# Runs in the evictions of q and k, value copies one unit later, a slot list in smaller doses and GpSimd in a pinned order

## The chip, the cores and the metric

The kernel runs on one core of a Trainium2 chip. The metric is device time in microseconds (us); lower is better. Three runs of the kernel before were timed, and one more execution was recorded with a profile.

## What is computed

Eight batches of banded attention are followed by a mixture of experts in which every token goes to one expert.

```python
# attention: B, H, S, D = 8, 8, 576, 64; heads 0-3: plain window of 32; heads 4-7: every 4th key of 128
scores = q @ k.T / 8; scores outside the band are masked; attn = softmax(scores)
x = (attn @ v) laid out as [B*S, H*D] = [4608, 512]
# experts: E = 8, F = 1024
logits = x @ w_gate + modality_bias[modality_id]
e = argmax(logits); g = softmax(logits)[e]
out = g * (relu(x @ w1[e]) @ w2[e])
```

## The kernel before

**Attention.** A batch is nine units (m = 0 to 8): four units of two tiles of 64 queries for the plain heads (kind 0), one mixed unit, and four units for the dilated heads (kind 1). One loop over t = 9b + m issues, at each t, a stage of several units: the scores of unit t (TensorE into the one tile `pss`, then VectorE adds the mask and takes the maximum, GpSimd subtracts it in `sm`), the exponent of unit t-1 (ScalarE), the transposition of the probabilities of t-2 (TensorE, evicted by ScalarE to `pT`), the product with the values of t-3 (`attend`, TensorE), the normalising and storing of t-3 and t-4 and the router's logits of t-5. ScalarE, VectorE, TensorE and SyncE (SP, which issues the loads) each run their instructions strictly in the order in which this loop writes them. GpSimd's order was left to a scheduler, apart from chains that were declared.

**q and k of the next batch** come as `st` tiles and are transposed in six chunks (`qk_chunks`), one for q and one for k in each of the three units m = 4, 5, 6 (kind 0) and m = 8, 0, 1 (kind 1). A chunk is four TensorE transpositions into one PSUM tile and one ScalarE eviction (two for kind 1) to `kT` or `qT`. In `qT` and `kT` the token p*6 + s lies at its own place, so the 96 columns of one transposition (one s) go to places six elements apart.

**Values.** `load_v` brings 64 rows of each tile to partitions 32 to 95 of `vw`; `shift_v`, a ScalarE copy of 32x520 for each head, copies the last 32 rows of each tile to the partitions 0 to 31 of the next one. `attend` of unit m = 0 runs at t with m = 3, that of unit m = 4 at m = 7.

**Experts.** From batch 4 on three early slots of up to 256 tokens are formed; the slots numbered 0 to 2 here. After the last batch the full list of slots is made (`gating`, `slot_info`, `slot_list`, `rest_info`: some 45 small VectorE instructions on one partition, run as a generator, a step for each `advance()`), and 15 more full slots and one half slot follow. A slot has 8 steps f. Each step is 12 matmuls with `w1` (L854), a ReLU (`hh` on ScalarE, `hl` on VectorE), splits of the next weights (`w1h`, `w2h` on ScalarE, `w1l`, `w2l` on VectorE, L802 and L803) and 6 matmuls with `w2` (L834). The tokens of a slot come through a chain: their indices (`idt`, a load by SP that needs the list), four indirect gathers by GpSimd into the one tile `xr`, a store to `x_slot` by SP, four loads into the one tile `xg` by SP, two transpositions `xt` by VectorE with splits `xh` (ScalarE) and `xl` (VectorE). The weights of the next slot are loaded by SP in six pieces, each of which waits until its place was used: `w2q` pair 0, `w1q` half 0, pairs 1 and 2, half 1, pair 3. `hold` at a slot's start issues what is missing of its inputs before its first matmul. After the loop over t, a short loop issues steps of the experts and of the list until the list is there (`state['routed']`).

Of the kernel before, what the change touches and what calls it, by code (L numbers as in the profile page):

```python
# [22 lines left out]
B, H, S, D = 8, 8, 576, 64  # L23
# [10 lines left out]
PQ = 96  # L34
SI = S // PQ
# [29 lines left out]
def kernel(  # L65
# [12 lines left out]
    nc = tc.nc  # L78
# [30 lines left out]
    def vw(b, kd):  # L109
        return vws[(2 * b + kd) % 3]  # L110

    def load_one(b, kd, src, queue=nc.sync):

        t = ald.tile([PQ, SI, 4, D], F32, name="st")
        for h in range(4):
            queue.dma_start(out=t[:, :, h], in_=src[b, 4 * kd + h].rearrange("(p s) d -> p s d", s=SI))
        return t

    def load_qk(b, kd, queue=nc.sync):
        kn = load_one(b, kd, k)  # L120
        return load_one(b, kd, q, queue), kn

    def load_v(b, kd, part=slice(None)):

        t = vw(b, kd)
        if kd == 0:
            nc.sync.dma_start(out=t[WIN:KW, :, :, 0:D], in_=v[b, 0:4].rearrange("h (i p) d -> p h i d", p=TQ))
        else:
            vv = v[b, 4:8].rearrange("h (j r) d -> r j h d", r=NCLS)
            for i, o, r, j, n in [(i, *seg) for i in range(NTILE) for seg in _csegs(TQ * i, TQ * (i + 1))][part]:  # L130
                nc.sync.dma_start(out=t[WIN + o:WIN + o + n, :, i, 0:D], in_=vv[r, j:j + n])
        return t

    def shift_v(b, kd, h):

        t = vw(b, kd)
        nc.scalar.copy(out=t[0:WIN, h, 1:NTILE].rearrange("p i d -> p (i d)"), in_=t[TQ:KW, h, 0:NTILE - 1].rearrange("p i d -> p (i d)"))

    state = {('qk', 0, 0): load_qk(0, 0, nc.scalar)}
# [3 lines left out]
    ident = cpool.tile([P, P], F32, name="ident")  # L143
# [125 lines left out]
    class InOrder:  # L269


        def __getattr__(self, name):
            def issue(*args, **kw):
                ins = tc.keep_in_program_order(getattr(nc.gpsimd, name)(*args, **kw))  # L274
                state['pool'] = ins.ins
                return ins
            return issue

    pool = InOrder()


    def qk_chunks(kd, qn, kn):


        def chunk(n, is_q):
            src = qn if is_q else kn
            pt = psum['o'].tile([P, 512], F32, name="po") if is_q and psum['many'] else ps_t.tile([P, 512], F32, name="pt")
            for g in range(2):
                for i in range(2):
                    nc.tensor.transpose(out=pt[:, PQ * (2 * g + i):PQ * (2 * g + i + 1)],  # L290
                                        in_=src[:, 2 * n + i, 2 * g:2 * g + 2].rearrange("p a d -> p (a d)"), identity=ident[:PQ, :PQ])
            flat = qT[kd] if is_q else kT[kd][:, :, WIN:]
            inp = pt[:, 0:4 * PQ].rearrange("c (g i p) -> c g i p", g=2, p=PQ)
            if kd == 0:
                parts = [(flat.rearrange("c g (p s) -> c g s p", s=SI)[:, :, 2 * n:2 * n + 2], inp)]
            else:

                parts = []
                for e in range(2):
                    o = 6 * e + 2 * n  # L300
                    dst = flat.rearrange("c g (r j t) -> c g r t j", r=NCLS, t=3)[:, :, o % 4:o % 4 + 2, o // 4]
                    parts.append((dst, inp.rearrange("c g i (j e) -> c g i e j", e=2)[:, :, :, e]))
            for dst, src in parts:
                if is_q:
                    nc.scalar.mul(dst, src, 1.0 / 8.0)
                else:
                    nc.scalar.copy(out=dst, in_=src)
        return [(lambda n=n, is_q=is_q: chunk(n, is_q)) for n in range(SI // 2) for is_q in (False, True)]
# [363 lines left out]
    order = []  # L672
# [4 lines left out]
    NU = len(order)  # L677
# [245 lines left out]
    def step(share=MOE_RATE / 6):  # L923

        nonlocal credit
        if moe:
            credit += share if state['t'] < NU else 1
            while credit >= 1:
                credit -= 1
                next(moe, None)  # L930

    def advance(some=range(-1, B)):
        for b, task in tasks:
            if b in some:
                next(task, None)

    state['routed'] = False
    for t in range(NU + LAG + 1):
        state['t'] = t
        if 'go' in state and not moe:  # L940
            octx.close()
            psum['many'] = False
            psum['y'] = ctx.enter_context(tc.tile_pool(name="ps_y", bufs=2, space=PSUM))
            psum['o'] = ctx.enter_context(tc.tile_pool(name="ps_o1", bufs=1, space=PSUM))
            moe = slots(NS, ids_of, ahead, hold)
        b, m = t // 9, t % 9
        if t == 1:
            pieces = qk_chunks(1, *state['qk', 0, 1])
        if t < NU:
            jobs = order[t][1]  # L950
            if m == 0:
                state['lT', b] = gwk.tile([2 * NE, S], F32, name="lT")
            if b + 1 < B:
                if m == 4:
                    pieces = qk_chunks(0, *state['qk', b + 1, 0])
                elif m == 8:
                    pieces = qk_chunks(1, *state['qk', b + 1, 1])
            if m == 0 and b > 0:
                load_v(b, 1, slice(6, None))
            elif m == 3:  # L960
                if b + 1 < B:
                    state['v', b + 1, 0] = load_v(b + 1, 0)
            units.append(Unit(b, m, jobs, [state['v', b, 0], state['v', b, 1]] if m >= 4 else [state['v', b, 0]], state['lT', b]))
            units[t].scores()
        step()
        if 0 <= t - 1 < NU:
            units[t - 1].exp()
        po = psum['o'].tile([P, 512], F32, name="po")
        if 0 <= t - 3 < NU:
            units[t - 3].attend(po)  # L970
        step()
        if 0 <= t - LAG < NU:
            units[t - LAG].logits(po)
        if 0 <= t - 3 < NU:
            units[t - 3].normalize()
        if 0 <= t - LAG < NU:
            units[t - LAG].gather_logits()
            if (t - LAG) % 9 == 8:
                tasks.append(((t - LAG) // 9, background((t - LAG) // 9)))
        step()  # L980
        advance()
        if 0 <= t - 2 < NU:
            units[t - 2].probsT()
        step()
        if 0 <= t - 4 < NU:
            units[t - 4].store()
            units[t - 4].keep(pool)

        if 3 <= m <= 6 and b < B:
            shift_v(b, 1, m - 3)  # L990
        elif t < NU and (m == 8 and b + 1 < B or m < 3):
            for h in ((m + 1) % 9,) if t > 2 else {0: (0, 1), 1: (2, 3), 2: ()}[t]:
                shift_v(b + (m == 8), 0, h)
        for i in range(2):
            step()
            if i < len(pieces):
                pieces[i]()
        pieces = pieces[2:]
        if t < NU and b + 1 < B:

            if m == 1:
                state['k', 1] = load_one(b + 1, 1, k)
            elif m == 2:
                state['qk', b + 1, 1] = load_one(b + 1, 1, q), state['k', 1]
            elif m == 6 and b + 2 < B:
                state['k', 0] = load_one(b + 2, 0, k)
            elif m == 7 and b + 2 < B:
                state['qk', b + 2, 0] = load_one(b + 2, 0, q), state['k', 0]
            elif m == 8:
                state['v', b + 1, 1] = load_v(b + 1, 1, slice(0, 6))  # L1010
        advance([*round_of, B - 1] if moe and t < NU else range(-1, B))


    while not state['routed']:
        step(1)
        advance()
        advance()
    run(moe)
    man.close()
# [34 lines left out]
```

## Time and profile before

| | |
|---|---|
| runs | 710.84, 721.43, 710.94 us; median 710.94 us |
| profiled execution | 717.6 us; span 715.9 us, so 1.7 us lie around the span |
| busy: TensorE, VectorE, ScalarE, GpSimd | 652.0, 496.2, 455.5, 290.7 us |
| granted TensorE clock, mean | 0.954 |

In the rows PE is TensorE's matmuls, PEld its weight loads, DVE VectorE, ACT ScalarE, POOL GpSimd, and SPq SyncE's queue. A row of the timeline gives start and duration in us, engine, line, operation, output <- inputs, shapes and count, and in brackets the idle time before it with what ended it. Attention fills about the first 258 us; the experts' slots start there and repeat every 22.56 us once they run alone.

### The profile page before, as it was taken

Reading aid. Unit: us, or ns where it says so; the run is one execution under the profiler, and the core shown is the slowest. Engines: PE = TensorE matmul, PEld = TensorE weight load, DVE = VectorE, ACT = ScalarE, POOL = GpSimd, SP = SyncE. Lnnn points to the kernel's source line nnn. Section 1 sums busy time; section 2 is a strip of 40 time slices with the busy share of each in tenths; the row PEclk is TensorE's granted clock in tenths of the full one; section 3 lists DMA queues with packets and bytes.
Section 4 is the critical chain, followed back from the end, with each engine's and each line's share of the span. In section 5 each row is a group of like instructions: output and inputs, shape, how many; then the busy total and the mean of one; then the engine's idle time right before and its main releaser. Section 6 shows DMA issues by size and latency. Waiting matters only on the chain. (4 is left out here: it accounts for less than half of the span.)

```text
span 715.9 us, 17885 instructions
## 1 busy us (share of the span) xinstructions
PE 652.0 (91%) x6286; PEld 572.8 (80%) x6286; DVE 496.2 (69%) x1212; ACT 455.5 (64%) x964; POOL 290.7 (41%) x396
## 2 busy tenths in 40 slices
PE   6898899996988789879999999999999999999991
PEld 3687777775876578779999989999999899999880
DVE  1678788785787788687666766677666776667660
ACT  4698799895767665436656555656665565665650
POOL 7344766764658654433333232333213231310110
PEclk7699999999789899989999999999999999999996
DMA  9897698697856964213333863233232336821730
GB/s 163 144 224 176 156 193 177 136 189 131 166 123 159 242 161 79 89 51 98 118 108 100 247 170 115 75 104 119 73 106 75 104 118 169 220 82 46 197 90 12
DMA packets 163233, 94.95 MB, mean 133 GB/s; under 512 B 124144, under 2 KB 143090, under 8 KB 163140
## 3 DMA queue, kind: packets, MB, share of 16 engines
q1 hardware_dynamic: 146612, 63.89, 40.1%
q0 software_dynamic: 11120, 28.64, 13.2%
q10 hardware_dynamic: 5408, 1.24, 1.1%
q8 instruction: 51, 0.84, 0.5%
q14 instruction: 42, 0.34, 0.2%
HBM read 127.52 MB, written 29.39 MB: 219 GB/s over the span
## 5 line engine op out<-in xcount | busy, mean ns | idle before, releaser
L854 PE MATMUL pt<-xh,w1l 128*128 128x256 f32 (+1 forms) x608 | 172.6, 284 | 7.5 <-DVE w1l L803 7.5
L854 PE MATMUL pt<-xl,w1h 128*128 128x256 f32 (+1 forms) x608 | 172.1, 283 | 0.0
L854 PE MATMUL pt<-xh,w1h 128*128 128x256 f32 (+1 forms) x608 | 172.0, 283 | 0.0
L860 ACT ACTIVATE hh<-pt 128x256 fp32r<-128x256 f32 (+1 forms) x152 | 57.6, 379 | 160.3 <-PE pt L854 160.2
L803 DVE TENSOR_TENSOR w2l<-w2q,w2h 128x512 fp32r<-128x512 f32 x152 | 104.8, 689 | 43.1 <-ACT w2h L802 34.7
L274 POOL DMA_INDIRECT xr<-x_dram,idt x74 | 82.8, 1118 | 121.4 <-DMA x_slot<-xr 70.5
L854 PEld LDWEIGHTS pt<-xh,w1l 128*128 128x128 f32 x608 | 116.5, 192 | 8.4 <-DVE w1l L803 8.4
L854 PEld LDWEIGHTS pt<-xh,w1h 128*128 128x128 f32 x608 | 116.4, 191 | 7.2 <-ACT w1h L802 0.6
L854 PEld LDWEIGHTS pt<-xl,w1h 128*128 128x128 f32 x608 | 116.4, 191 | 5.7
L834 PE MATMUL py<-w2h,hh 128*128 128x512 f32 x296 | 118.3, 400 | 0.0
L834 PE MATMUL py<-w2h,hl 128*128 128x512 f32 x296 | 117.2, 396 | 0.0
L834 PE MATMUL py<-w2l,hh 128*128 128x512 f32 x296 | 116.2, 393 | 0.0
L861 DVE SCALAR_TENSOR_TENSOR hl<-pt,hh 128x256 fp32r<-128x256 f32 (+1 forms) x152 | 63.2, 416 | 74.9 <-ACT hh L860 74.9
L274 POOL DMA_INDIRECT out_dram<-ys,idt x37 | 39.8, 1076 | 178.7 <-ACT ys L837 115.8
L803 DVE TENSOR_TENSOR w1l<-w1q,w1h 128x512 fp32r<-128x512 f32 x152 | 103.8, 683 | 3.0 <-ACT w1h L802 3.0
L802 ACT CAST w1h<-w1q 128x512 fp32r<-128x512 f32 x152 | 94.5, 622 | 3.6 <-DMA w1q<-in_moe_w_dram 3.6
L802 ACT CAST w2h<-w2q 128x512 fp32r<-128x512 f32 x152 | 93.1, 612 | 0.0
L274 POOL TENSOR_TENSOR sm<-sm,nmx 128x384 f32<-128x384 f32 x72 | 59.9, 832 | 64.4 <-DVE den L368 49.3
L361 PE MATMUL po<-vw,pT 96*64 96x65 f32 x1152 | 55.9, 239 | 20.3 <-ACT pT L355 16.5
L361 PEld LDWEIGHTS po<-vw,pT 96*64 96x64 f32 x1152 | 44.6, 147 | 32.7 <-ACT pT L355 20.9
L834 PEld LDWEIGHTS py<-w2l,hh 128*128 128x128 f32 x296 | 55.9, 189 | 13.3
L834 PEld LDWEIGHTS py<-w2h,hh 128*128 128x128 f32 x296 | 56.4, 190 | 6.7
(160 smaller groups left out, 1119.9 us busy)
## 6 DMA issues: line engine op xcount, KB each, us to landing
w2q<-in_moe_w_dram SPq DMA_DIRECT2D x76, 512.0 KB
w1q<-in_moe_w_dram SPq DMA_DIRECT2D x152, 256.0 KB
st<-in_k_dram SPq DMA_DIRECT2D x64, 144.0 KB
x_slot<-xr SPq DMA_DIRECT2D x18, 512.0 KB
xg<-x_slot SPq DMA_DIRECT2D x72, 128.0 KB
x_dram<-x_sb POOLq DMA_DIRECT2D x32, 256.0 KB, 3.6
st<-in_q_dram SPq DMA_DIRECT2D x56, 144.0 KB
vw<-in_v_dram SPq DMA_DIRECT2D x8, 576.0 KB
```

Source lines behind the costliest of these rows:

```text
L274: ins = tc.keep_in_program_order(getattr(nc.gpsimd, name)(*args, **kw))
L361: nc.tensor.matmul(out=pov[u * TQ:(u + 1) * TQ, h, :], lhsT=self.pT[:, h, u * TQ:(u + 1) * TQ], rhs=self.vts[kd][:, h, i, :], start=True, ...
L802: nc.scalar.copy(out=hi, in_=raw)
L803: nc.vector.tensor_tensor(out=lo, in0=raw, in1=hi.bitcast(F32), op=ALU.subtract)
L834: nc.tensor.matmul(out=py[u], lhsT=ht[:, us], rhs=wt, start=(f + n == 0), stop=(f + n == FC + 1))
L854: nc.tensor.matmul(out=ph, lhsT=wt[:, c, :], rhs=xt[:, c, 0:cols], start=(c + i == 0), stop=(c + i == KC + 1))
L860: nc.scalar.activation(out=hh, in_=ph, func=AF.Relu)
L861: nc.vector.scalar_tensor_tensor(out=hl, in0=ph, scalar=0.0, in1=hh.bitcast(F32), op0=ALU.max, op1=ALU.subtract)
```

## The change

There are four edits.

1. **Evictions of kind 0.** The four transpositions of a chunk write PSUM with a step of 4 (or 2) elements, so that four (two) tokens that are neighbours in `qT`/`kT` lie beside each other. The eviction reads PSUM in one contiguous run and writes runs of 4 (2) elements, still at a step of six from run to run. The chunks 0 and 1 take one pair of heads each with s = 0 to 3, chunk 2 both pairs with s = 4, 5; before, every chunk took both pairs with two s. Kind 1 keeps its patterns.
2. **Value copies.** For kind 0 the four copies stood at m = 8, 0, 1, 2 and stand at m = 0, 1, 2, 2; for kind 1 they stood at m = 3, 4, 5, 6 and stand at m = 4, 5, 6, 6.
3. **Slot list.** The last loop issued one step of the experts and two of the list at a time; now it is three steps of the experts and one of the list.
4. **GpSimd.** Each instruction issued through `pool` is tied behind the one before it in the scheduler's eyes. No semaphore is added.

```diff
         def __getattr__(self, name):
             def issue(*args, **kw):
                 ins = tc.keep_in_program_order(getattr(nc.gpsimd, name)(*args, **kw))
+                if 'pool' in state:
+                    tc.add_manual_dep(ins.ins, state['pool'].name, mybir.DependencyInfo(mybir.DependencyClass.NoSync, mybir.DependencyReason.SCHED_ONLY),
+                                      reason="GpSimd's order")
                 state['pool'] = ins.ins
...
-            for g in range(2):
-                for i in range(2):
-                    nc.tensor.transpose(out=pt[:, PQ * (2 * g + i):PQ * (2 * g + i + 1)],
-                                        in_=src[:, 2 * n + i, 2 * g:2 * g + 2].rearrange("p a d -> p (a d)"), identity=ident[:PQ, :PQ])
             flat = qT[kd] if is_q else kT[kd][:, :, WIN:]
-            inp = pt[:, 0:4 * PQ].rearrange("c (g i p) -> c g i p", g=2, p=PQ)
+            inp = pt[:, 0:4 * PQ]
             if kd == 0:
-                parts = [(flat.rearrange("c g (p s) -> c g s p", s=SI)[:, :, 2 * n:2 * n + 2], inp)]
+                gs, s0, ns = ((n,), 0, 4) if n < 2 else ((0, 1), 4, 2)
+                inp = inp.rearrange("c (g p i) -> c g p i", g=len(gs), i=ns)
+                jobs = [(inp[:, x, :, i], s0 + i, g) for x, g in enumerate(gs) for i in range(ns)]
+                parts = [(flat[:, gs[0]:gs[-1] + 1].rearrange("c g (p s) -> c g p s", s=SI)[:, :, :, s0:s0 + ns], inp)]
...
+            for to, i, g in jobs:
+                nc.tensor.transpose(out=to, in_=src[:, i, 2 * g:2 * g + 2].rearrange("p a d -> p (a d)"), identity=ident[:PQ, :PQ])
...
-        if 3 <= m <= 6 and b < B:
-            shift_v(b, 1, m - 3)
-        elif t < NU and (m == 8 and b + 1 < B or m < 3):
-            for h in ((m + 1) % 9,) if t > 2 else {0: (0, 1), 1: (2, 3), 2: ()}[t]:
-                shift_v(b + (m == 8), 0, h)
+        for h in {0: (0,), 1: (1,), 2: (2, 3)}.get(m, ()) if 2 < t < NU else {0: (0, 1), 1: (2, 3)}.get(t, ()):
+            shift_v(b, 0, h)
+        for h in {4: (0,), 5: (1,), 6: (2, 3)}.get(m, ()) if t < NU else ():
+            shift_v(b, 1, h)
...
     while not state['routed']:
-        step(1)
-        advance()
+        for _ in range(3):
+            step(1)
         advance()
```

What this does to the order of the engines is shown at three places.

GpSimd in batch 7, before: `sm` is the subtraction that the softmax of a unit waits for, `xr` are the gathers of slot 1, `table` a scatter of the router.

```order
L274 DMA x_dram_84<-x_sb 64x256
L274 DMA x_dram_85<-x_sb 64x256
L493 DMA table<-pay,dst 41472x3
L274 DMA xr<-x_dram_84,idt 128x256
L274 DMA xr<-x_dram_85,idt 128x256
L274 DMA xr<-x_dram_84,idt 128x256
L274 TENSOR_TENSOR sm<-sm,nmx 128x384
```

The same engine after the change, at the end of batch 7, where the last `sm` of all stands:

```order
L274 TENSOR_TENSOR sm<-sm,nmx 128x384
L274 DMA x_dram_84<-x_sb 64x256
L274 DMA x_dram_85<-x_sb 64x256
L274 DMA xr<-x_dram_84,idt 128x256
L274 DMA xr<-x_dram_85,idt 128x256
L274 DMA xr<-x_dram_84,idt 128x256
L274 DMA xr<-x_dram_85,idt 128x256
```

The gathers of slot 1 have moved from ahead of subtractions, with nine subtractions still to come, to behind the last one.

VectorE in slot 1, before, where the list is computed (`w2l` and `w1l` are the splits that the matmuls need, `hl` the VectorE half of a ReLU, the rest belongs to the list):

```order
L548 SCALAR_TENSOR_TENSOR cs<-one_277,ns 1x8
L559 TENSOR_TENSOR ge<-sidx,cs 1x200
L561 TENSOR_REDUCE es<-ge 1x25
L563 TENSOR_TENSOR ns<-full,done 1x8
L565 TENSOR_TENSOR ge<-ge,ns 1x200
L567 TENSOR_REDUCE bs<-ge 1x25
```

The same instructions after the change, at the end of slot 1 (the first `hl` here is that of its step 7, the second that of step 0 of slot 2):

```order
L555 SCALAR_TENSOR_TENSOR cs<-one_277,ns 1x8
L868 SCALAR_TENSOR_TENSOR hl<-pt,hh 128x256
L566 TENSOR_TENSOR ge<-sidx,cs 1x200
L568 TENSOR_REDUCE es<-ge 1x25
L570 TENSOR_TENSOR ns<-full,done 1x8
L810 TENSOR_TENSOR w2l<-w2q_245,w2h 128x512
L810 TENSOR_TENSOR w1l<-w1q_240,w1h 128x512
L868 SCALAR_TENSOR_TENSOR hl<-pt,hh 128x256
```

The list stood in two blocks around the `hl` of step 3 of slot 1, 30 instructions of it in the second; now 2 to 14 of them stand between one `hl` and the next. The list of the full slots is complete behind the `hl` of step 1 of slot 2, where it was complete ahead of the `hl` of step 4 of slot 1.

SP before, where the tokens of slot 3 (the first slot that needs the list) are stored; `w2q_245` is pair 3 of slot 2's weights, and the `idt` here is that of slot 5:

```order
L665 DMA w2q_245<-in_moe_w_dram 128x2x512
L620 TENSOR_LOAD info_5924
L620 ISA x2
L622 ISA
L622 DMA idt<-table 128x6
L641 DMA x_slot<-xr 128x2x512
```

SP after, at the same store; `w2q_244` is here pair 2 of slot 3's own weights, `w1q_241` the first load of their half 1:

```order
L672 ISA
L672 DMA w2q_244<-in_moe_w_dram 128x2x512
L648 DMA x_slot<-xr 128x2x512
L669 ISA
L669 DMA w1q_241<-in_moe_w_dram 32x4x512
```

The store of slot 3 has moved from behind the weights of slot 2 to behind four of the six pieces of slot 3's weights. The load of slot 3's indices has moved likewise, from behind pair 1 to behind pair 3 of slot 2's weights. On GpSimd the gathers of slot 3 stood ahead of the two scatters of slot 1's output to `out` and now stand behind them. The splits `xt`, `xh`, `xl` of slot 3, which were spread over steps 3 to 6 of slot 2, now stand together between the last step of slot 2 and the first of slot 3.

More of the change, by code (lines that the diff above doesn't have):

```diff
@@ L287, in chunk @@
             pt = psum['o'].tile([P, 512], F32, name="po") if is_q and psum['many'] else ps_t.tile([P, 512], F32, name="pt")
-            for g in range(2):
-                for i in range(2):
-                    nc.tensor.transpose(out=pt[:, PQ * (2 * g + i):PQ * (2 * g + i + 1)],
-                                        in_=src[:, 2 * n + i, 2 * g:2 * g + 2].rearrange("p a d -> p (a d)"), identity=ident[:PQ, :PQ])
             flat = qT[kd] if is_q else kT[kd][:, :, WIN:]
-            inp = pt[:, 0:4 * PQ].rearrange("c (g i p) -> c g i p", g=2, p=PQ)
+            inp = pt[:, 0:4 * PQ]
             if kd == 0:
-                parts = [(flat.rearrange("c g (p s) -> c g s p", s=SI)[:, :, 2 * n:2 * n + 2], inp)]
-            else:
+                gs, s0, ns = ((n,), 0, 4) if n < 2 else ((0, 1), 4, 2)
+                inp = inp.rearrange("c (g p i) -> c g p i", g=len(gs), i=ns)
+                jobs = [(inp[:, x, :, i], s0 + i, g) for x, g in enumerate(gs) for i in range(ns)]
+                parts = [(flat[:, gs[0]:gs[-1] + 1].rearrange("c g (p s) -> c g p s", s=SI)[:, :, :, s0:s0 + ns], inp)]
+            else:
+                inp = inp.rearrange("c (g i p) -> c g i p", g=2, p=PQ)
+                jobs = [(inp[:, g, i], 2 * n + i, g) for g in range(2) for i in range(2)]
                 parts = []
```

## Prediction

> **What bounds the kernel now.** I read the page's totals first, then the table by stage, then single rows.
>
> ```profile
> span 715.9 us, 17885 instructions
> ...
> PE 652.0 (91%) x6286; PEld 572.8 (80%) x6286; DVE 496.2 (69%) x1212; ACT 455.5 (64%) x964; POOL 290.7 (41%) x396
> ```
>
> TensorE leads, with 64 us of the span idle. The execution took 717.6 us, 1.7 beyond its span. The stages (from:to, length, busy time of PE, PEld, DVE, ACT, POOL, then the granted clock, the DMA share and GB/s) show where the 64 us lie:
>
> ```profile
> 102.00:129.00 27.00, 24.97 (x457) 21.31 (x451) 22.73 (x77) 24.74 (x55) 19.22 (x30) 1.00 0.87 184
> ...
> 168.00:176.00 8.00, 3.54 (x63) 2.93 (x56) 2.31 (x8) 1.10 (x4) 2.57 (x4) 1.00 0.42 102
> 176.00:186.00 10.00, 9.10 (x85) 8.36 (x86) 6.37 (x22) 8.60 (x18) 2.90 (x5) 0.50 1.10 170
> ...
> 228.00:241.00 13.00, 9.66 (x134) 8.00 (x126) 7.33 (x23) 7.30 (x19) 11.03 (x13) 0.74 0.90 174
> ...
> 304.00:312.00 8.00, 3.92 (x14) 3.62 (x15) 7.47 (x29) 2.00 (x4) 2.62 (x4) 0.61 0.03 2
> ...
> 340.00:705.00 365.00, 359.39 (x2297) 324.75 (x2296) 251.63 (x443) 216.29 (x447) 96.26 (x87) 1.00 0.43 120
> ```
>
> A steady batch of attention (102 to 129) has TensorE and ScalarE both within 2.3 us of its 27. Three holes follow, each with a reduced clock in it or behind it: at 168, 228 and 304. From 340 to 705 TensorE is full (359.39 of 365). No edit touches work there, so what is won or lost lies ahead of 340.
>
> **Evictions.** In kind 0, ScalarE needs 118.10 to 121.53 = 3.43 us from one exponent to the next with a q and a k eviction between them; TensorE's share of the batch, 24.97 us over nine units, is 2.77 a unit. ScalarE is the longer one there.
>
> ```profile
> 118.10 0.52 ACT L347 ACTIVATE pe<-sm 128x384 f32<-128x384 f32 x1
> ...
> 119.00 0.37 ACT L387 CAST uxh<-pt 128x256 fp32r<-128x256 f32 x1
> ...
> 121.53 0.53 ACT L347 ACTIVATE pe<-sm 128x384 f32<-128x384 f32 x1
> ```
>
> ```profile
> L305 ACT ACTIVATE qT<-po 128x384 f32<-128x384 f32 x24 | 21.9, 912 | 0.0
> ...
> L307 ACT COPY kT<-pt 128x384 f32<-128x384 f32 x24 | 20.6, 857 | 1.1 <-PE pt L290 1.1
> ...
> L307 ACT COPY kT<-pt 128x192 f32<-128x192 f32 x48 | 16.1, 413 | 0.1
> ```
>
> Contiguous, 384 elements took 0.52 and 256 took 0.37: 1.2 ns an element and 0.06 fixed. The kind 0 eviction (every element 24 bytes from the last) costs 2.08 ns an element, that of kind 1 (12 bytes) 1.84. So it is the break between elements that costs, about 0.87 ns. No row has runs of 4. One break in 4 gives 0.22 ns an element, 0.08 for 384, so kT takes 0.61; one in 2 gives 0.69. Against 0.857 a chunk saves 0.25, 0.25 and 0.17, and q the same: 1.34 us a batch. The bounds are 0 and 2.2 (three pairs at the contiguous 0.52). TensorE is 0.66 behind in such a unit and the loads take 0.87 of the DMA's time, so I take 1.1 of the 1.34. Batch 5 does its chunks at half clock behind the hole at 168, which leaves six batches: **-6.5** (-11 to 0). The first chunk of the program needs only one pair of heads: -1 (-2 to 0).
>
> **Value copies.** The list of ScalarE's copies has three that waited for the load, each the copy at m = 3:
>
> ```profile
> 87.27 0.62 ACT L137 COPY vw<-vw 32x520 f32<-32x520 f32 x1 [2.76 <-DMA vw<-in_v_dram]
> ...
> 141.90 0.63 ACT L137 COPY vw<-vw 32x520 f32<-32x520 f32 x1 [0.92 <-DMA vw<-in_v_dram]
> ...
> 175.21 0.62 ACT L137 COPY vw<-vw 32x520 f32<-32x520 f32 x1 [6.88 <-DMA vw<-in_v_dram]
> ...
> 176.90 1.14 PE L361 MATMUL po<-vw,pT 96*64 96x65 f32 x16 [5.33 <-ACT pT L355]
> ```
>
> Behind the waiting copy stand the exponent and the evictions of the next units, and for them waits TensorE (5.33 us at 176.90). The copies at m = 4 come one unit, 2.75 us, later. That covers 2.75, 0.92 and 2.75, 6.4 in all. The last two copies now share a unit, closer ahead of the `attend` that reads them; a load that is over by then costs nothing there, a later one shows as before. I take **-5** (-6.4 to -2). Of the hole at 168 four microseconds stay, and with them, likely, the half clock until 186.
>
> **GpSimd's order.** Ahead of one subtraction stand a scatter and three gathers of slot 1:
>
> ```profile
> 228.63 1.09 POOL L274 DMA_INDIRECT xr<-x_dram,idt  x1 [0.30 <-DVE uxl L388]
> ...
> 233.25 0.52 ACT L347 ACTIVATE pe<-sm 128x384 f32<-128x384 f32 x1 [3.71 <-POOL sm L274]
> ```
>
> ScalarE waits 3.71 us for that subtraction and the clock falls to 0.74 over 228 to 241. With the gathers behind the last subtraction this goes. In exchange the tokens of slot 1 come later by the nine units less what the chain has in hand; slot 0 runs meanwhile, and I cost it at +1. Together **-3** (-5 to +1).
>
> **Smaller doses.** In slot 1 VectorE works at the list in one piece, TensorE waits, and its clock over 304 to 312 is 0.61.
>
> ```profile
> 299.64 0.15 DVE L523 TENSOR_SCALAR cn<-po 1x8 int32<-1x8 f32 x1
> ...
> 308.07 0.58 PE L854 MATMUL pt<-xh,w1l 128*128 128x256 f32 x1 [5.23 <-DVE w1l L803]
> ```
>
> The wait of 5.23 and the reduced clock (0.39 of 8 us, less the idle part: about 2.3) make 7.5. The 45 small instructions at 0.15 are not gone: 7 us in ten steps in which VectorE has about 0.9 us to spare each (251.63 of 365 is busy). A step with 14 of them is over by 1.2, so I leave +1.5: **-6** (-7.5 to -4.5).
>
> **The new wait.** The list is now complete later, and slot 3 is the first to need it. Times from here are counted from the first ReLU of slot 2. A slot's rows show the pace, and the rows behind them the steps of the chain.
>
> ```profile
> 364.83 1.03 POOL L274 DMA_INDIRECT xr<-x_dram,idt  x1 [9.93 <-DMA x_slot<-xr]
> ...
> 365.17 0.39 ACT L860 ACTIVATE hh<-pt 128x256 fp32r<-128x256 f32 x1 [1.41 <-PE pt L854]
> ...
> 369.27 1.00 POOL L274 DMA_INDIRECT xr<-x_dram,idt  x1 [0.30 <-issue]
> ...
> 380.91 0.07 SPq L665 DMA_DIRECT2D w2q<-in_moe_w_dram  x1
> ...
> 387.73 0.39 ACT L860 ACTIVATE hh<-pt 128x256 fp32r<-128x256 f32 x1 [1.41 <-PE pt L854]
> ...
> 395.74 1.14 POOL L274 DMA_INDIRECT out_dram<-ys,idt  x1 [2.50 <-ACT w1h L802]
> ```
>
> ```profile
> 218.68 1.05 POOL L274 DMA_INDIRECT xr<-x_dram,idt  x1 [0.30 <-issue]
> ...
> 222.55 0.40 SPq L641 DMA_DIRECT2D x_slot<-xr  x1
> ...
> 286.06 0.39 SPq L641 DMA_DIRECT2D x_slot<-xr  x1
> ...
> 308.55 1.56 SPq L622 DMA_DIRECT2D idt<-table  x2
> ...
> 311.45 1.06 POOL L274 DMA_INDIRECT xr<-x_dram,idt  x1 [4.77 <-DMA idt<-table]
> ...
> 326.38 1.81 SPq L647 DMA_DIRECT2D xg<-x_slot  x4
> ...
> 331.75 0.71 DVE L786 STREAM_TRANSPOSE xt<-xg 128x512 f32<-128x512 f32 x1 [1.02 <-DMA xg<-x_slot]
> ```
>
> ```profile
> L792 ACT CAST xh<-xt 128x512 fp32r<-128x512 f32 x37 | 23.0, 621 | 7.6 <-DVE info L583 6.0 <-DVE xt L786 1.5
> L793 DVE TENSOR_TENSOR xl<-xt,xh 128x512 fp32r<-128x512 f32 x37 | 25.3, 684 | 1.2 <-ACT xh L792 1.2
> ```
>
> A slot lasts 387.73 - 365.17 = 22.56, a step 2.82. The list is done behind step 1's ReLU and seven instructions at 0.15: +4.8. SP issues `idt` at +6 to +7, and 2.9 later (308.55 to 311.45) the gathers could start, at +9 to +10. The scatters of slot 1 stand ahead of them and end at 396.88 - 387.73 = +9.15 at the earliest. Four gathers (364.83 to 370.27) take 5.44: +14.9. The store can go 2.8 behind the last (219.73 to 222.55): +17.7, which is behind the weights that it now follows (380.91 - 365.17 = +15.74). The loads come 2.8 later by the gap from a store to its loads (`xg` follows at 288.86 the store of 286.06):
>
> ```profile
> 288.86 1.31 SPq L647 DMA_DIRECT2D xg<-x_slot  x3
> ```
>
> So +20.5; `xt` 5.4 later (326.38 to 331.75): +25.9. Two transpositions, two `xh` and one `xl` in turn make 3.3: +29.2. TensorE wants them at 22.56 - 1.41 = +21.15. The wait is **8.0**; with the shortest values of each step 6.3, with a second scatter that holds GpSimd up 12. All of TensorE's other work stands behind it, in order. Behind such a wait the clock has fallen before (5.33 idle, then 0.50 for ten microseconds, which cost about 5; the hole at 304 cost 2.3): +2.5 (0 to 5). Together **+10.5** (+6 to +17). The Trainium skill, "TensorE: Matmul & The Clock Gate", Part 1: The HAM clock gate, has the rate halved after an idle window of about 3.4 us and restored after a busy one of that length. By it this part would be about +1.7 (an estimate, half of a window), and the sum 0.8 lower; the row 176 to 186 shows half rate for far longer than that.
>
> **Sum:** -6.5 - 1 - 5 - 3 - 6 + 10.5 = -11, so 706.6 against the 717.6 of the profiled execution. Two of three timed runs before lie 6.7 below that execution, about the size of the 6.88 wait at 175.21, so I take them as runs without that hole. There the copies save 2.75 less: -8, and 710.94 - 8 = **703**.
>
> **Rivals.** *No late slot 3*: the chain has slack that I do not see, say the scatters or the weights let it pass. Against it stand the order of SP and the 22.56 us of a slot. Without the 10.5 it is 703 - 10.5 = 692.
>
> *The evictions give nothing*: the ScalarE time is not shorter, or TensorE and the loads (0.87) take its place. For it speaks that TensorE is only 2.0 us short of a batch. Without the 6.5: 709.
>
> *The change makes transpositions slower, and the kernel with them.* The PSUM writes of kind 0 go 16 or 8 bytes apart.
>
> ```profile
> 115.08 0.50 PE L290 MATMUL pt<-ident,st 96*128 96x96 f32 x4
> ...
> 115.41 0.49 PE L290 MATMUL po<-ident,st 96*128 96x96 f32 x4
> ```
>
> Four of them take 115.41 - 115.08 = 0.33 now, 0.083 each. In attention 7 batches x 6 chunks x 4 = 168 are such; d more for each costs 168 d. From d = 0.048 the forecast's -8 is gone and the kernel is slower than before; twice the time (0.083) gives +14 and 717, four times 745. Nothing in the trace strides an fp32 output of TensorE, so neither end is excluded. The Trainium skill has such a rule in "Advanced Engine Details and Errata", Memory Cachelines: PSUM lines hold two FP32 values, and an access that is not contiguous slows matmuls a lot. No row here shows it.
>
> **How the numbers follow.** The forecast as summed gets 0.50 (696 to 710), no late slot 0.15 (692), no gain of the evictions 0.20 (709), slow transpositions 0.12 (717 and up), anything else 0.03. The range leaves out a tenth at either end: 689, a little under the no-late-slot case with its bounds, to 716, where the slow transpositions begin. Two per cent, about what a measurement of this kernel can tell from no change, is 14.2 us: below 696.7 is faster, above 725.2 slower. Faster holds the second case and a fifth of the first: 0.25. Slower needs transpositions of 2.6 times the time or more: 0.05. The rest, 0.70, is within 2%.
>
> **What the profile after would show.** `kT` evictions of kind 0 near 0.61 to 0.69, and a steady batch of about 26 us instead of 27; no ScalarE wait over 1 us for `vw` but the one at 175, there about 4; no gather between the subtractions of batch 7, and no 0.74 behind 228; no wait of 5 us for `w1l` in slot 1, but one of 6 to 12 for `xh` or `xl` at the first matmul of slot 3. I am wrong if a batch stays at 27, if slot 3 starts on time, or if four transpositions take over 0.5 us.

## The result and the profile after

The changed kernel takes 723.31 us (median of 20 runs) against 713.38 for the kernel before, measured in turn with it: ratio 1.0114, 95% interval 1.0088 to 1.0140. The ratio leaves out the few runs in a slower state that each kernel has now and then, and the two medians lie 9.9 us apart. By the ratio the change is slower by about 8 us where 8 us faster was forecast. The profiled execution took 725.8 us, that of before 717.6. The totals of the changed kernel's page:

```profile
span 724.1 us, 17881 instructions
...
PE 653.8 (90%) x6286; PEld 573.0 (79%) x6286; DVE 496.8 (69%) x1212; ACT 438.3 (61%) x964; POOL 295.6 (41%) x396
```

TensorE has the same work; ScalarE has 17 us less of it (455.5 before), and that bought nothing. In a table by stage a row gives from:to, length, busy time of PE, PEld, DVE, ACT and POOL, then the granted clock, the DMA share and GB/s. This one is over the stretches shown of before:

```profile
102.00:129.00 27.00, 24.29 (x390) 20.56 (x388) 19.70 (x66) 19.44 (x48) 16.09 (x26) 0.87 0.92 169
...
168.00:176.00 8.00, 7.97 (x147) 6.79 (x146) 6.76 (x23) 5.54 (x13) 4.83 (x8) 1.00 0.55 131
176.00:186.00 10.00, 8.53 (x155) 7.11 (x152) 8.66 (x37) 8.12 (x21) 6.15 (x13) 1.00 1.11 222
...
228.00:241.00 13.00, 9.04 (x124) 6.96 (x125) 8.55 (x25) 7.33 (x15) 5.60 (x7) 0.75 0.91 222
...
304.00:312.00 8.00, 8.00 (x54) 7.25 (x53) 7.69 (x24) 3.98 (x9) 2.10 (x2) 1.00 0.06 5
...
340.00:705.00 365.00, 359.14 (x2268) 324.64 (x2268) 248.94 (x438) 213.58 (x441) 98.05 (x86) 0.99 0.41 118
```

The holes at 168 and 304 are gone, the one at 228 is not (0.75, before 0.74). The first row is no steady batch here: batch 3 lasts 30.3 us with the clock at 0.89. Batches 1 and 2 last 26.7 and 26.8, where the undisturbed ones of before last 27.0 and 26.7 and about 26 was forecast. The last row looks as full as before (359.14 of 365), but it holds 2268 matmuls where it held 2297: part of that busy time is at a lower clock. The slots, each from its first ReLU to that of the next, tell it plainly (us):

| slot | starts | 0 | 1 | 2 | 3 | 6 | 15 | every other full slot |
|---|---|---|---|---|---|---|---|---|
| before | 261.5 | 25.8 | 32.8 | 22.6 | 22.6 | 23.3 | 22.6 | 22.4 to 22.6 |
| after | 254.5 | 29.7 | 24.0 | 32.9 | 23.8 | 27.0 | 27.3 | 22.4 to 22.6 |

Slots 1 to 3 lose 2.8 together, as a smaller copy of the forecast (+4.5). Slots 0, 6 and 15 lose 3.9, 3.7 and 4.8: for slot 0 +1 was forecast, for the other two nothing. Slot 0 starts 7.0 earlier; what of that is the change's is left to the experiments. The windows of slots 2, 3, 6 and 15 of the changed kernel:

```profile
308.20:341.00 32.80, 24.36 (x145) 21.64 (x144) 19.41 (x50) 13.79 (x28) 11.62 (x10) 0.88 0.32 101
341.00:364.90 23.90, 23.90 (x146) 21.46 (x145) 16.03 (x28) 13.62 (x29) 8.06 (x7) 0.94 0.25 84
410.00:437.00 27.00, 24.36 (x145) 21.69 (x144) 15.99 (x28) 13.60 (x28) 8.45 (x8) 0.94 0.69 176
617.50:644.80 27.30, 24.45 (x145) 21.70 (x145) 15.92 (x28) 13.61 (x28) 8.45 (x8) 0.94 0.65 157
```

And the group of TensorE's first matmuls of each step, with what it waited for in the last two columns: the 8.3 us are the forecast wait of slot 3 (8.0), the 5.3 are new and lie in slots 6 and 15.

```profile
L861 PE MATMUL pt<-xh,w1h 128*128 128x256 f32 x576 | 165.8, 288 | 13.6 <-ACT xh L799 8.3 <-ACT w1h L809 5.3
```

**What makes slot 6 late** is to be read on GpSimd, SP and ScalarE in slot 5 (it starts at 387.4 in the changed kernel, at 387.7 before). The timeline of the changed kernel, GpSimd first:

```profile
395.46 1.13 POOL L274 DMA_INDIRECT out_dram<-ys,idt  x1 [2.51 <-ACT w1h L809]
396.90 1.55 POOL L274 DMA_INDIRECT xr<-x_dram,idt  x1 [0.30 <-issue]
398.75 1.02 POOL L274 DMA_INDIRECT xr<-x_dram,idt  x1 [0.31 <-issue]
...
397.55 0.39 SPq L672 DMA_DIRECT2D w2q<-in_moe_w_dram  x1
406.40 0.39 SPq L648 DMA_DIRECT2D x_slot<-xr  x1
407.49 0.37 SPq L672 DMA_DIRECT2D w2q<-in_moe_w_dram  x1
...
421.79 0.62 ACT L809 CAST w1h<-w1q 128x512 fp32r<-128x512 f32 x1 [5.06 <-DMA w1q<-in_moe_w_dram]
```

The same places before:

```profile
397.83 0.39 SPq L665 DMA_DIRECT2D w2q<-in_moe_w_dram  x1
398.40 0.41 SPq L641 DMA_DIRECT2D x_slot<-xr  x1
403.47 0.37 SPq L665 DMA_DIRECT2D w2q<-in_moe_w_dram  x1
...
419.43 0.62 ACT L802 CAST w1h<-w1q 128x512 fp32r<-128x512 f32 x1 [2.42 <-DMA w1q<-in_moe_w_dram]
```

After the scatters of slot 4 (the last at 395.46) come two more gathers, those of the second half of a slot that is being collected. The store `x_slot` needs the data of all four. The last gather is issued by 399.77, and the DMA engines are full until 404 (share 1.03 to 1.07 in the stretches from 398). The list of SP's waits from 384 to 425 (total, times, longest) has the store's wait for the gathers, and the same list of before has none:

```profile
SPq L648 <- DMA xr<-x_dram,idt: 8.3, 1, 8.3
```

So SP stands at the store until 406.40, where it passed at 398.40, and the next piece of weights goes at 407.49 instead of 403.47. From 404 to 406 the DMA share (the last but one column) is 0.21 after, 0.92 before:

```profile
404.00:406.00 2.00, 2.00 (x13) 1.74 (x13) 1.52 (x4) 1.63 (x4) 0.00 (x0) 1.00 0.21 66
```

```profile
404.00:406.00 2.00, 2.00 (x14) 1.74 (x13) 1.52 (x4) 1.35 (x4) 0.00 (x0) 1.00 0.92 327
```

The weights arrive only where the expert changes: SP's queue moves 2.7 to 3.6 MB in each of the slots 5, 6, 14, 15 and 17 of the kernel before and 0.5 to 1.6 MB in the slots between them, since the load of an unchanged expert is skipped. There the DMA engines are nearly full, and the kernel before lost 0.7 us in slot 6 as it was. What the idle stretch of the DMA engines delays is paid for by ScalarE (5.06 at 421.79), by TensorE (2.6), and by a lower clock after it (1.8 us more of busy time in slot 6).

### The profile page after: what moved, and what is told of

Same layout as the page of the kernel before. It is cut to its first block, busy times and chain, and to the rows that moved or that the text cites. A ratio compares the mean times of both kernels' runs of the same rounds, so it can differ in the third digit from the quotient of the medians.

```text
span 724.1 us, 17881 instructions
## 1 busy us (share of the span) xinstructions
PE 653.8 (90%) x6286; PEld 573.0 (79%) x6286; DVE 496.8 (69%) x1212; ACT 438.3 (61%) x964; POOL 295.6 (41%) x396
## 5 line engine op out<-in xcount | busy, mean ns | idle before, releaser
L861 PE MATMUL pt<-xh,w1h 128*128 128x256 f32 (+1 forms) x608 | 174.2, 287 | 13.6 <-ACT xh L799 8.3
L861 PE MATMUL pt<-xl,w1h 128*128 128x256 f32 (+1 forms) x608 | 173.9, 286 | 0.1
L861 PEld LDWEIGHTS pt<-xh,w1h 128*128 128x128 f32 x608 | 118.1, 194 | 21.7 <-ACT xh L799 8.7
L274 POOL DMA_INDIRECT xr<-x_dram,idt x74 | 86.0, 1162 | 120.1 <-DMA x_slot<-xr 94.4
L861 PEld LDWEIGHTS pt<-xl,w1h 128*128 128x128 f32 x608 | 118.1, 194 | 6.1 <-DVE xl L800 0.4
L861 PEld LDWEIGHTS pt<-xh,w1l 128*128 128x128 f32 x608 | 118.1, 194 | 2.4 <-DVE w1l L810 2.4
L362 ACT COPY pT<-pt 96x512 f32<-96x512 f32 x72 | 41.5, 576 | 40.2 <-PE pt L359 37.7
```

What stands on the lines that cost most here:

```text
L362: nc.scalar.copy(out=self.pT, in_=src)
L861: nc.tensor.matmul(out=ph, lhsT=wt[:, c, :], rhs=xt[:, c, 0:cols], start=(c + i == 0), stop=(c + i == KC + 1))
```

## The experiments

Each ran beside the kernel before on one chip; ratios are to that, with 95% intervals.

**Each edit alone.** Evictions:

```diff
-                parts = [(flat.rearrange("c g (p s) -> c g s p", s=SI)[:, :, 2 * n:2 * n + 2], inp)]
+                parts = [(flat[:, gs[0]:gs[-1] + 1].rearrange("c g (p s) -> c g p s", s=SI)[:, :, :, s0:s0 + ns], inp)]
```

> Before with the evictions of kind 0 alone. Theory (TensorE bounds a steady batch, 24.9 of 27 us busy): the evictions are near 0.49 us, ScalarE is 2.2 us less busy in a batch, and a steady batch is shorter by 0.3 us only; the whole is 0 to 3 us faster than before, and slots 1, 3, 6 and 15 last what they last before (32.8, 22.6, 23.3, 22.6). Rival (ScalarE bounds these units, as predicted): a steady batch near 26 us, the whole about 6.5 us faster.

Ratio 0.9994 (0.9958 to 1.0030). ScalarE's groups and two transpositions in a row, here from the changed kernel, which has the same lines:

```profile
L312 ACT ACTIVATE qT<-po 128x384 f32<-128x384 f32 x24 | 11.9, 497 | 0.4
L314 ACT COPY kT<-pt 128x384 f32<-128x384 f32 x24 | 11.7, 486 | 1.2 <-PE pt L309 1.0
```

```profile
90.37 0.49 PE L309 MATMUL pt<-ident,st 96*128 96x96 f32 x4
90.70 0.49 PE L309 MATMUL po<-ident,st 96*128 96x96 f32 x4
```

The evictions fell from 857 and 912 ns to 486 and 497, more than forecast, and the transpositions stayed at 0.33 for four. With the evictions alone the batches 1, 2 and 3 last 26.9, 26.7 and 27.3 us, where the undisturbed ones of before last 27.0 and 26.7. A shorter ScalarE did not make them shorter.

Value copies:

```diff
-        if 3 <= m <= 6 and b < B:
-            shift_v(b, 1, m - 3)
+        for h in {4: (0,), 5: (1,), 6: (2, 3)}.get(m, ()) if t < NU else ():
+            shift_v(b, 1, h)
```

> Before with the value copies one unit later alone. Theory: the ScalarE waits for values of 1 to 7 us shrink by up to one unit of 2.75 us each; the whole is 2 to 5 us faster, the slots as before. Rival: the loads are late by amounts that differ between executions, and the whole is within 2 us.

Ratio 1.0015 (0.9984 to 1.0045): the rival. GpSimd's tie:

```diff
+                if 'pool' in state:
+                    tc.add_manual_dep(ins.ins, state['pool'].name, mybir.DependencyInfo(mybir.DependencyClass.NoSync, mybir.DependencyReason.SCHED_ONLY),
```

> Before with GpSimd's instructions tied in order alone. Theory: the tie costs in two places. In batch 6 a gather of slot 0 that waits for its indices stands ahead of a subtraction: ScalarE waits some 6 us there; what batch 7 saves (3.7) does not make up for it. And in every later slot the two scatters stand between the second and the third gather of a slot, so the store of its tokens is issued later, SP is late with the weights behind it, and slots 6 and 15, before which an expert's weights change, last 26 to 27 us instead of 23.3 and 22.6: 6 to 10 us slower in all. Rival (the later list made slots 6 and 15 longer, not the tie): they last 23.3 and 22.6, and the whole is 0 to 3 us faster.

Ratio 1.0102 (1.0060 to 1.0143): a loss as large as that of the whole change. Slot 0 lasts 26.8, slot 6 27.8, slot 15 24.9, slots 1 to 3 what they lasted before. Its window of slot 6, and TensorE's waits in the same group as above, where no `xh` is left but the `w1h` are:

```profile
406.70:434.50 27.80, 24.63 (x145) 21.66 (x145) 15.96 (x28) 13.60 (x28) 8.86 (x8) 0.94 0.68 176
```

```profile
L857 PE MATMUL pt<-xh,w1h 128*128 128x256 f32 x576 | 164.4, 285 | 4.6 <-ACT w1h L805 4.5
```

Smaller doses:

```diff
-        step(1)
-        advance()
+        for _ in range(3):
+            step(1)
         advance()
```

> Before with the smaller doses alone. Theory: slot 1 is some 9 us shorter (32.8 to about 24) and slot 2 with 3 some 11 us longer together, because slot 3 cannot start before its tokens, which follow the list: 1 to 4 us slower in all, slots 6 and 15 as before (23.3 and 22.6). Rival (the later list also delays the chain of all later slots): slots 6 and 15 last 26 to 27 us, 9 to 12 us slower in all.

Ratio 0.9980 (0.9950 to 1.0011). In the profile the theory holds: slots 1, 2, 3 last 24.0, 32.9 and 24.0, 80.9 instead of 77.9, and slots 6 and 15 22.9 and 22.6. The 3 us do not show in the whole, which the spread of the attention part covers: slot 0 starts between 251 and 262 us in the profiles of kernels with the old evictions. Its group row shows the wait that has only moved (before: 7.1 for `w1l`, none for `xh`):

```profile
L854 PE MATMUL pt<-xh,w1h 128*128 128x256 f32 x576 | 164.5, 286 | 8.4 <-ACT xh L792 8.3
```

**Where the tie costs.** The changed kernel with the gathers written two at a time:

```diff
                                         bounds_check=nrows - 1, oob_is_err=False)
-                yield
+            yield
         yield
```

In the tied order of the changed kernel the scatters of slot 4 come after 30 gathers, so between the halves of a slot (4 each); here they come after 32, as in the kernel before.

> The changed kernel, tie included, with the gathers of a slot written two at a time, so that in the tied order all four stand ahead of a slot's two scatters again. Theory (the scatters between the second and third gather are what delays the stores, SP and the weights): slots 6 and 15 go from 27.0 and 27.3 back to 22.6 to 23.5, and the whole is 6 to 9 us faster than the changed kernel, within 3 us of before. Rival (the tie costs by itself, wherever the scatters stand): slots 6 and 15 stay at 25 to 27, 5 to 10 us slower than before.

Ratio 1.0022 (0.9986 to 1.0057). Slots 6 and 15 last 22.56 both, better than before; slot 0 keeps its length (30.0). The window of slot 6 has TensorE busy throughout, and in the group only slot 3's wait is left:

```profile
403.10:425.70 22.60, 22.60 (x145) 20.47 (x145) 16.01 (x28) 13.73 (x29) 8.12 (x8) 1.00 0.72 179
```

```profile
L861 PE MATMUL pt<-xh,w1h 128*128 128x256 f32 x576 | 164.3, 285 | 8.5 <-ACT xh L799 8.4
```

The store goes at 389.85, 9.3 after the start of slot 5, where the changed kernel has 19.0 and the kernel before 10.7. The tie is kept; the split alone was the cause of the loss in slots 6 and 15. Tied in attention only, and in the experts only:

```diff
-                if 'pool' in state:
+                if 'pool' in state and 'go' not in state:
```

```diff
-                if 'pool' in state:
+                if 'pool' in state and 'go' in state:
```

> The changed kernel with GpSimd's tie only until the experts take over, at the end of batch 7. Theory: slots 6 and 15 at 22.6 to 23.5, as in the kernel of the doses alone; what the tie does in attention comes to nothing (a wait of some 6 us in batch 6 for one of some 4 in batch 7): within 4 us of before. Rival (the tie's loss lies in attention): 5 to 10 us slower than before.

> The changed kernel with GpSimd's tie only from the end of batch 7 on. Theory: slots 6 and 15 at 25 to 27.5, the whole 5 to 10 us slower than before. Rival (the tie's loss lies in attention): slots 6 and 15 the same but the whole within 3 us of before, or those slots at 22.6 to 23.5.

Ratios 0.9980 (0.9956 to 1.0005) and 1.0115 (1.0038 to 1.0193, four runs). With the tie in attention only, slots 0, 6 and 15 last 25.8, 23.7 and 22.6; with it in the experts only 29.1, 27.1 and 26.9. So slot 0's loss is the tie's as well: the gathers of slot 1 stand behind the last subtraction, and `xt` of slot 1 comes 15.8 us after slot 0 starts (16.5 in the changed kernel) instead of 12.9.

"Attention only" does not hold to the end of batch 7, however. The flag `go` is set at the last unit but one, and the gathers of slot 1 are issued after that, so they are not tied. In this run they still stand ahead of a subtraction, and ScalarE waits for it as in the kernel before (3.71):

```profile
221.68 1.00 POOL L274 DMA_INDIRECT xr<-x_dram,idt  x1 [0.30 <-issue]
222.69 0.84 POOL L274 TENSOR_TENSOR sm<-sm,nmx 128x384 f32<-128x384 f32 x1
...
223.57 0.52 ACT L354 ACTIVATE pe<-sm 128x384 f32<-128x384 f32 x1 [3.69 <-POOL sm L274]
```

The run shows no cost of the tie up to there; what it gains in batch 7 it cannot show.

**Evictions and copies again, and together**, all three on one chip.

> The evictions alone once more, beside the copies alone and both together on one chip. Theory (the two parts act on the same ScalarE queue in attention and only together take its waits off TensorE): 0 to 2 us faster than before. Rival (the parts simply add): half of what both together gain, 2 us or more.

> The value copies alone once more. Theory (they help only with shorter evictions ahead of them): between 2 us faster and 3 us slower than before. Rival (the parts add): 2 us or more faster.

> Evictions and copies of the change together, nothing else of it. Theory: 3 to 6 us faster than before, all of it ahead of slot 0; slots 0 to 18 as before (25.8, 32.8, then 22.6 each, 23.3 in slot 6). Rival (neither does anything; the earlier starts of slot 0 in single profiles were chance): within 2 us.

Ratios 0.9989 (0.9954 to 1.0025), 1.0045 (1.0015 to 1.0074) and 0.9993 (0.9964 to 1.0022). Together they do nothing that can be measured, so the theory of the last one is wrong; the copies alone cost 1 to 5 us, at the upper end of what their theory allowed. Slot 0's start 7.0 us sooner in the profile after the change is left open. The slots take 15.2 us more there, the part behind them 34.3 in both, and the whole loses 8. Chance accounts for 1.7 of the 7.0 (an estimate: the profiled execution of before took 4.2 us more than its median, that of the changed kernel 2.5); for the rest no run gives a cause. The waits list of the copies alone, from 40 to 260 us (total, times, longest), and the row of before for the same wait:

```profile
PEld po L361 <- ACT vw L137: 6.8, 18, 0.5
PE po L361 <- ACT vw L137: 4.3, 18, 0.4
ACT vw L137 <- DMA vw<-in_v_dram: 1.1, 1, 1.1
```

```profile
PE po L361 <- ACT vw L137: 0.9, 4, 0.2
```

The waits for the load have gone in this kernel (1.1 in place of 10.6), but each copy now stands right ahead of the product that reads it, and TensorE waits for it 18 times. Batches 2 and 3 last 27.6 each, where undisturbed ones last 27.0 and 26.7 before.

The waits for the load do not stay away, though. The same list has them with the evictions alone and in the changed kernel, which has the copies one unit later:

```profile
ACT vw L137 <- DMA vw<-in_v_dram: 7.1, 4, 3.3
```

```profile
ACT vw L137 <- DMA vw<-in_v_dram: 8.5, 4, 3.2
```

They differ from profile to profile: in the other kernels with both edits they come to between nothing (two steps, below) and 7.4 us (both edits alone). Batch 3 of the changed kernel, the one of 30.3 us, has such a wait of 2.96.

**Doses between the two.** Evictions and copies, no tie, and two steps or one for each step of the list:

```diff
-        step(1)
-        advance()
+        step(1)
+        step(1)
         advance()
```

```diff
-        advance()
         advance()
```

> Evictions and copies of the change, no tie, and in the last loop two steps of the experts for one of the list in place of three for one: the list is complete at the end of slot 1 instead of after step 1 of slot 2. Theory (slot 3 starts 28 to 29 us after the list is there, whoever waits meanwhile, so an earlier list in small doses gains): slot 1 about 24, slot 2 with the wait for slot 3 24 to 27, so slots 1 to 3 last 70 to 73 us together instead of the 77.9 before: 5 to 8 us faster than before. Rival (the wait just changes place, whatever the doses): slots 1 to 3 at 77 or more, within 2 us of before.

> Evictions and copies of the change, no tie, and one step of the experts for one of the list. Theory (slot 3 follows the list by 28 to 29 us, or its own place in the order of slot 2 if that is later): the list is there about 21 us after slot 1 starts instead of 25 with two steps, slot 1 lasts 26 to 28, slots 1 to 3 together 74 to 76, and the whole is 5 to 8 us faster than before. Rival (denser doses bring VectorE's stall of slot 1 back, nothing is left): slots 1 to 3 at 77 or more.

Ratios 0.9944 (0.9915 to 0.9974) and 0.9932 (0.9901 to 0.9963): both are faster than the kernel before, by a little less than the 5 to 8 us expected. With two steps slots 1 to 3 last 76.8 (25.8, 28.0, 23.0), not 70 to 73. With one they last 75.7 (29.7, 23.5, 22.6): the sum as expected, but slot 1 longer and slot 2 shorter than expected: a part of VectorE's stall is back, and TensorE waits 4.2 us for `w1l`. The last instruction of the list of the full slots and the first ReLU of slot 3, in the changed kernel and with two steps:

```profile
312.81 0.16 DVE L605 TENSOR_TENSOR info<-ec 1x25 int32<-1x25 f32 x1
...
341.05 0.38 ACT L867 ACTIVATE hh<-pt 128x256 fp32r<-128x256 f32 x1 [3.54 <-PE pt L861]
```

```profile
295.77 0.17 DVE L602 TENSOR_TENSOR info<-ec 1x25 int32<-1x25 f32 x1
...
324.77 0.38 ACT L864 ACTIVATE hh<-pt 128x256 fp32r<-128x256 f32 x1 [4.09 <-PE pt L858]
```

From the end of that instruction slot 3 follows the list by 28.1 and 28.8 us, as the theory says. What failed with two steps was the time of the list: 24.9 after slot 1's start, since its first instruction stands at 12 to 14 us in all these kernels. For 70 to 73 it would have been needed at about 20; slot 3 was 3 us sooner than after the change, no more. Of the 4 to 5 us that these two kernels gain, the slots 1 to 3 show 1.1 and 2.2; the rest is not assigned, and the intervals reach down to 1.8 and 2.6.

## Why the prediction was wrong

- **"No edit touches work there" (340 to 705)** is the step that failed. The change's fourth edit was weighed at one place of the program, the subtractions of batch 7, though it ties GpSimd's order to the end. In every later slot it put the two scatters between the halves of a slot's gathers, so SP stood 8.3 us at a store with the next weights behind it, and slots 6 and 15 lost 3.7 and 4.8 us where nothing was forecast. The kernel with the tie alone loses 7.3 us (4 to 10); with the gathers in pairs, tie kept, slots 6 and 15 lose nothing and the whole is at 1.0022. The prediction counted what stands behind a waiting instruction on SP for slot 3, where it was right, and did not ask it for the slots in steady state.
- **GpSimd's order in attention (-3)**. The wait of 3.71 in batch 7 is gone in all four kernels in which the gathers of slot 1 are tied. In the changed kernel a longer one stands in batch 6: the gather of slot 0 waits 8.48 us for its indices, the subtraction stands behind it, and ScalarE waits 6.82.

```profile
206.67 1.09 POOL L274 DMA_INDIRECT xr<-x_dram,idt  x1 [8.48 <-DMA idt<-table]
207.77 0.77 POOL L274 DMA_DIRECT2D x_dram<-x_sb  x1
208.55 0.85 POOL L274 TENSOR_TENSOR sm<-sm,nmx 128x384 f32<-128x384 f32 x1
...
209.43 0.52 ACT L354 ACTIVATE pe<-sm 128x384 f32<-128x384 f32 x1 [6.82 <-POOL sm L274]
```

  The experiment with the tie alone was expected to show this as a price of the tie. That order is not the tie's: the kernel before has it too (the gather waits 3.26, ScalarE 1.04), and so has, without any tie, the kernel with the copies alone:

```profile
207.74 1.10 POOL L274 DMA_INDIRECT xr<-x_dram,idt  x1 [6.99 <-DMA idt<-table]
...
210.51 0.52 ACT L347 ACTIVATE pe<-sm 128x384 f32<-128x384 f32 x1 [4.63 <-POOL sm L274]
```

  The gather's wait differs from profile to profile, from 2.2 to 8.5 us. And the clock over 228 to 241 is as low as before (0.75): VectorE now stands there 2.34 us at the tokens of slot 0, and TensorE waits 1.10 and 1.75 for results of VectorE behind it. What the tie is worth in attention stays open: no run ties batch 7 and leaves the slots behind it alone. Slot 1's later tokens, put at +1, cost 3.3 to 4.2 with the rest of the change and 1.0 with the tie alone.
- **Evictions (-6.5 and -1)**: the rival came true. The durations were better than forecast (saving 0.79 for a pair, not 0.45); the kernel gains 0.4 to 0.8 (nothing, within the interval). Batch 1, where ScalarE hardly waits for values, is 0.1 and 0.5 shorter in the two profiles of the evictions alone, with TensorE busy 25 of its 27. In the batches behind it ScalarE waits for the load of the values, 1.4, 1.9 and 3.3 us in the first of these profiles. So both things that the prediction named with this rival, TensorE and the loads, show up; how much is each one's, no run separates. The mistake was to compare ScalarE's 3.43 of one unit with TensorE's mean of 2.77 and to call ScalarE the bound of it, when units with less ScalarE work follow and catch up: behind the exponent at 121.53 come the next ones after 3.5 and then 1.2.
- **Value copies (-5)**: with the copies alone the waits for the load went as forecast. In the changed kernel they did not: there are four, 8.5 in all, where one of over 1 us was to be left. And the price of the nearer deadline, put at nothing when the load is over by then, was the copy itself ahead of the product: 0.24 us in 18 units. Alone +1 to +3, with the shorter evictions ahead of them about 0.
- **Smaller doses (-6) and the new wait (+10.5)**: the mechanism holds. The steps of the chain came where the sum put them: counted from the first ReLU of slot 2, the store at +17.6 (forecast 17.7), the loads at +20.4 (20.5), `xt` at +25.9 (25.9), the first matmul at +29.4 (29.2). TensorE waited 8.29 (8.0):

```profile
337.56 0.58 PE L861 MATMUL pt<-xh,w1h 128*128 128x256 f32 x1 [8.29 <-ACT xh L799]
```

  Slots 1 to 3 together: +2.8 after the change, +2.9 with the doses alone, against +4.5. The difference lies in slot 1, which lasts 8.8 less, not 6: at 32.8 against 22.6 it had lost 10.2, of which the sum counted 7.5. Slots 2 and 3 lost 11.6, the wait and 3.3 of clock (2.5 was forecast). Of the 3.3 only 1.3 show in slot 3; the other 2.0 lie ahead of its first ReLU and so in slot 2. The Trainium skill's "TensorE: Matmul & The Clock Gate", Part 1: The HAM clock gate, gave about 1.7 as an estimate; the trace has twice that, as the clock stayed at 0.50 for some six microseconds of unbroken matmuls.
- **Slower transpositions**, the rival on the slow side, did not come: 0.33 for four, as before. By the rule of the Trainium skill's "Advanced Engine Details and Errata", Memory Cachelines, they would have slowed; the trace disagrees.
- **The base**: the hole at 168 in the profile of before, which the sum's terms rested on in part, came from a wait of 6.88 for a load. In the profiles of other kernels with the old copies no such wait is over 3.8; a term read from one execution's late load is not the kernel's.

## What to carry to other kernels

An edit that pins an engine's order acts to the end of the program: compare the order in the steady loop, not only at the place that it is meant for, and ask for each instruction that waits for another engine what stands behind it in that queue and the next. A wait taken from one place comes back at the next deadline if the data behind it is as late as before; what helps is to have the data sooner, as the two doses between the extremes do (1.1 and 2.2 us in slots 1 to 3; the whole gains 4 to 5). A shorter operation on one engine gains little where TensorE's own busy time fills 92% of the stage, and the time that it frees may go into that engine's next wait, here the one for the values. Before a run is read as a part of the change, see in its trace that the order at the place in question is the one meant.

## What the runs showed of the hardware

- fp32 transpositions that write PSUM at a step of 16 or 8 bytes took the time of contiguous ones: 0.33 us for four in both.
- An eviction of 128x384 whose writes go in runs of two or four elements, 24 bytes from run to run, took 0.49, no more than the contiguous 0.52 of the exponent; single elements 24 bytes apart took 0.86 to 0.91. The price per break, worked out as 0.87 ns, does not hold for runs.
- Behind TensorE's wait of 8.29 us the granted clock was 0.50 from its first matmul at 337.56 to about 343.7, with matmuls in unbroken succession, and 1.00 from 344 on, a loss of 3.3 us; in the profile of before, behind a wait of 5.33, it was 0.50 for ten microseconds.
